# Seven block products for eight in the second feed-forward product of the last chunk

## The chip, the cores and the metric

The kernel runs on one core of a Trainium2 chip. The metric is the device time of one execution in microseconds (us), as the median of several runs. Engines are called as in the profile: PE is the matrix engine (PEld its weight loads), DVE the vector engine, ACT the scalar engine, POOL the GpSimd engine, SP the engine that issues most of the DMAs.

## What is computed

Two layers, each of a sliding attention and a feed-forward product, on 2048 rows of 576 numbers. Both layers use the same weights.

```python
def attention(x, wqkv, wo):          # 32 heads of 18, window of 8 keys, every second row
    q, k, v = split(x @ wqkv)
    logits = q . k[pos - 2 * w] * 18 ** -0.5     # w = 0..7, masked where pos - 2w < 0
    return (softmax(logits) . v) @ wo

def feed_forward(x, w1, w2):         # w1 is 576 x 4608, w2 is 4608 x 576
    return silu(x @ w1) @ w2

for layer in range(2):
    x = x + attention(layernorm(x), wqkv, wo)
    x = x + feed_forward(layernorm(x), w1, w2)
```

## The kernel before

**Stages.** The work is cut into eight chunks, `s` = 0 to 7: four of layer one, four of layer two, each of 512 rows, held as four blocks of 128 rows. `front(s)` makes a chunk's norm, its attention, the projection and a second norm; then comes its feed-forward part. Chunk seven is the last one, and its feed-forward part has no other work beside it. All matmuls take numbers split in two float16 parts, high and low, and add three terms: high by high, high by low, low by high.

**Feed-forward.** Chunks 0 and 1 use plain products (`ffn`). From chunk 2 on `ffn_pairs` takes the 36 tiles of 128 hidden columns as 18 pairs. The first product of a pair is a block product of 2x2 by 2x2 blocks, made with seven block multiplications for eight: `forms` builds seven combinations of the normed rows (split on ACT and DVE, turned by DMA, tiles `xf`, nine of them in the area `xb`), and `prepare` has built seven combinations of w1 per pair, once, kept in device memory (`wfs`) and loaded by `load_wf` into twelve tiles. Each of the products P1 to P7 is seven matmuls of 128x256 (line 1096). Their sums need copies out of the four PSUM banks `zz`: `snap` on ACT (L1100) and `add` on DVE (L1103). SiLU follows on ACT (L1119, L1121, L1123), and then the split of 4x256 hidden numbers into high and low: ACT L1126, DVE L1129.

**The second product** (`second`) runs over groups of three pairs. For each of the four row blocks it adds up 3 pairs x 2 tiles x 3 terms in a PSUM tile `acc`, in two halves of 288 columns (L1151), and DVE adds the sum to x (L861, at the very end L1160). Its weights are tiles of w2, high and low, loaded whole by `load_w2` (L871) into eleven tiles.

**What sets the order.** Each step is handed to `Plan` with an engine, an expected length, what it reads and writes, and a priority; `Plan.order` walks through a model of the engines, lets each free engine take the ready step of lowest priority number, and gives out tile places as they become free. What comes out is a fixed order of instructions on each engine's queue. On the chip an instruction that waits holds all behind it on its queue. Priorities are `s - 1.0` for a chunk's front, `s - 0.5` for feed-forward steps off PE and `s + 0.5` upward for those on PE. So attention and norms of chunk s+1 are worked into the feed-forward part of chunk s.

**Areas.** Tiles of different stages share memory (`area`, `part`, `parts`): a tile can be taken only when no live tile overlaps it. `xa` holds the normed rows for attention, and in the norm before feed-forward also the half `yb` of the combinations; `kvs` holds two tiles of keys and values; `prs` the products of attention; `o` its output or the other half `ya`; `wq` the QKV weights of layer two and two of three tiles `hq`.

Of the kernel before, what the change touches and what calls it, by code (L numbers as in the profile page):

```python
# [264 lines left out]
def sliding_attention_silu_ffn(ctx: ExitStack, tc: tile.TileContext, x, wqkv, wo, w1, w2, out):  # L265
# [10 lines left out]


# [3 lines left out]
    def T(b):  # L281
        return S.tags[b.tag][b.slot]
# [45 lines left out]
    part("yb", XA, 1, [8, KH], F32, turns=False)  # L328
# [15 lines left out]
    parts("yf", [(YH, 0), (YO, 0)], [2, KB], F16)  # L344
# [6 lines left out]
    part("w2", W2A, W2N, [2, D], F16)  # L351
# [64 lines left out]
    dz = accw[:, NP:NP + NP // 2, :].rearrange("p a b -> p (a b)")  # L416
    pace = cp.tile([1, 1], F32, name="pace")
# [57 lines left out]
    highs = []  # L475
    turned = []
# [21 lines left out]
    def layer_norm(xs, prio, into, on_act, on_pe=False, late=[]):  # L498
# [77 lines left out]
    def raw_wq(u):  # L576
# [3 lines left out]
        raw = lambda k: fl(T(rs[k]).bitcast(F32))[:, :QR]  # L580
# [132 lines left out]
    def attention(s, xT, wq, more=None):  # L713
# [4 lines left out]
        for u in range(NU):  # L718
            kv, qt = Buf("kv"), Buf("qt")
            own = [(kv, j) for j in range(NJ)]  # L720
            if wq is None:
# [8 lines left out]
            else:  # L730
                w = wq(u)
                if blk == 0:
# [3 lines left out]
                    op("POOL", 1.86, clear, [], [(kv, "edge")], pr_)  # L736
                else:
# [5 lines left out]
                    op("SP", 0.8, edge, [("eds", lay, par, u)], [(kv, "edge")], pr_, nbytes=20000, lanes=2)  # L743
                for j in range(NJ):
# [31 lines left out]
            keys = own + [(kv, "halo"), (kv, "edge")]  # L776
            lg, pe, mx, sm = Buf("lg"), Buf("pe"), Buf("mx"), Buf("mx")
            for j in range(0, NJ, 2):
# [9 lines left out]
                op("DVE", 2.49, mul, keys + [(qt, j), (qt, j + 1)], [pr], pr_)  # L788
                op("DVE", 2.49, red, [pr], [(lg, j)], pr_)
# [14 lines left out]
            op("DVE", 1.42 if blk == 0 else 0.98, soft_a, [], lgs + [mx], pr_)  # L804
            op("ACT", 0.36, lambda pe=pe, lg=lg: nc.scalar.activation(T(pe), T(lg), AF.Exp, scale=DH ** -0.5),
               lgs, [pe], pr_ - 0.2, table="exp")
            op("DVE", 1.38, soft_b, [], [pe, sm], pr_)
            for j in range(0, NJ, 2):
                pr = Buf("pr")

                for a in range(2):
# [5 lines left out]
                    op("DVE", 1.28, mul, keys + [pe], [(pr, a)], pr_, after=formed[-1:])  # L817
# [6 lines left out]
                op("DVE", 2.55, tree, [], [(pr, 0), (pr, 1), (o, j, u), (o, j + 1, u)], pr_, after=formed[-1:])  # L824
                if s == 0:
                    marks.append(op("POOL", 1.3, lambda j=j, u=u: nc.gpsimd.tensor_copy(
                        pace, T(o)[0:1, j, u * UC:u * UC + 1]), [(o, j, u)], ["pace"], -5))
# [69 lines left out]
    def raw_split(f0, prio):  # L897
# [10 lines left out]
        def rb(f):  # L908
            return fl(T(raws[f][1]).bitcast(F32))
# [428 lines left out]
```

## Time and profile before

| what | value |
|---|---|
| runs | 2142.57 us median of 3 (2138.58 to 2148.47) |
| span of the profiled execution | 2139.6 us; the record has no other time of it |
| POOL, busy in the span | 365.9 us (17%) |
| data moved by DMA | 426.21 MB, mean 199 GB/s |
| matmuls of the second product in chunks 2 to 7 (L1151) | 5184, 669.0 us busy, 286 ns each |
| matmuls of the first product there (L1096) | 5292, 671.2 us busy, 273 ns each |

A matmul's 286 ns is its own length; matmuls follow each other faster than that, since one starts while the one before drains. The time from start to start is read from a stretch of the chain of work with its count of matmuls. In the view of waits, a line names who waited, for whom, the sum in us, how many times, and the longest.

### The profile page before, as it was taken

Reading aid. Unit: us, or ns where it says so; the run is one execution under the profiler, and the core shown is the slowest. Engines: PE = TensorE matmul, PEld = TensorE weight load, DVE = VectorE, ACT = ScalarE, POOL = GpSimd, SP = SyncE. Lnnn points to the kernel's source line nnn. Section 1 sums busy time; section 2 is a strip of 40 time slices with the busy share of each in tenths; the row PEclk is TensorE's granted clock in tenths of the full one; section 3 lists DMA queues with packets and bytes.
Section 4 is the critical chain, followed back from the end, with each engine's and each line's share of the span. In section 5 each row is a group of like instructions: output and inputs, shape, how many; then the busy total and the mean of one; then the engine's idle time right before and its main releaser. Section 6 shows DMA issues by size and latency. Waiting matters only on the chain.

```text
span 2139.6 us, 41351 instructions
## 1 busy us (share of the span) xinstructions
PE 2114.5 (99%) x16233; PEld 1576.2 (74%) x16233; DVE 1640.1 (77%) x2599; ACT 977.0 (46%) x1803; POOL 365.9 (17%) x585
## 2 busy tenths in 40 slices
PE   8999899999999999999999999999999999999999
PEld 5556466656667888877788777887788877888887
DVE  8999999999977997548975599746997569853322
ACT  7555787644254553344424344343443434333332
POOL 2223656234242430001100010000000000000000
PEclk9999999999999999999999999999999999999999
DMA  6576777677799987775748765596565965566551
GB/s 182 154 228 245 250 262 247 197 266 237 197 234 287 325 248 209 175 214 167 211 121 224 201 180 160 138 248 190 157 175 146 250 178 165 162 156 199 152 169 62
DMA packets 334235, 426.21 MB, mean 199 GB/s; under 512 B 145608, under 2 KB 262708, under 8 KB 330072
## 3 DMA queue, kind: packets, MB, share of 16 engines
q1 hardware_dynamic: 293720, 293.19, 49.5%
q0 software_dynamic: 38304, 129.28, 18.8%
q8 instruction: 127, 2.08, 0.4%
q10 hardware_dynamic: 2016, 1.11, 0.2%
q14 instruction: 68, 0.56, 0.1%
HBM read 307.32 MB, written 67.68 MB: 175 GB/s over the span
## 4 chain that ended last, share of the span: by engine, by line
PE 88%; DMA 6%; DVE 3%; issue 1%; ACT 1%; SPq 1%; POOL 0%; ACTq 0%; DVEq 0%; POOLq 0%
PE acc L1151 28%; PE z L1096 13%; PE misc L1096 13%; PE z L1193 9%; PE acc L1212 9%; PE z L682 7%; PE acc L854 5%; PE misc L682 5%; DMA w<-wfs 1%; DMA xb<-yo 1%; DMA h<-in_A_wqkv_dram 1%; DMA w<-in_B_w_dram 1%; DMA w<-w2s 1%; DMA yo<-yh 0%; DMA x<-xd 0%
## 5 line engine op out<-in xcount | busy, mean ns | idle before, releaser
L1151 PE MATMUL acc<-w,h 128*128 128x288 f16 x5184 | 669.0, 286 | 1.6 <-DVE x L861 1.0
L1151 PEld LDWEIGHTS <-h 128*128 128x128 f16 x5184 | 507.2, 98 | 126.8 <-issue 2.2
L1096 PEld LDWEIGHTS <-w 128*128 128x128 f16 x5292 | 517.3, 98 | 72.0 <-DMA w<-wfs 3.7
L1096 PE MATMUL z<-xb,w 128*128 128x256 f16 x2653 | 335.5, 273 | 2.3 <-DMA w<-wfs 1.7
L1096 PE MATMUL misc<-xb,w 128*128 128x256 f16 x2639 | 335.7, 273 | 1.1 <-DVE hs L1103 0.9
L861 DVE SCALAR_TENSOR_TENSOR x<-acc,d,x 128x576 f32<-128x576 f32 x183 | 148.5, 812 | 129.8 <-PE acc L1151 122.2
L1212 PE MATMUL acc<-w,h 128*128 128x288 f16 x1728 | 215.4, 286 | 0.0
L682 PEld LDWEIGHTS <-xa 128*128 128x128 f16 x1344 | 131.0, 98 | 112.9 <-issue 2.1
L1212 PEld LDWEIGHTS <-h 128*128 128x128 f16 x1728 | 168.4, 98 | 44.2
L782 DVE TENSOR_TENSOR prs<-qt,kvs 128x2304 f32<-128x2304 f32 x64 | 163.4, 2552 | 10.3 <-DMA kvs<-kvs 9.4
L815 DVE TENSOR_TENSOR prs<-kvs,pe 128x1152 f32<-128x1152 f32 x128 | 170.8, 1351 | 0.5
L786 DVE TENSOR_REDUCE lg<-prs 128x128 f32<-128x2304 f32 x64 | 163.0, 2547 | 1.0
L822 DVE TENSOR_TENSOR prs<-prs 128x1152 f32<-128x1152 f32 (+1 forms) x128 | 135.1, 1055 | 3.1
L1129 DVE SCALAR_TENSOR_TENSOR h<-wq,sh,h 128x1024 f16<-128x1024 f32 x60 | 76.8, 1280 | 73.3 <-ACT h L1126 73.3
L1193 PE MATMUL z<-xb,w 128*128 128x512 f16 x588 | 129.1, 379 | 3.3 <-ACT w L931 1.6
L682 PE MATMUL z<-wq,xa 128*128 128x432 f16 x658 | 124.4, 346 | 0.0
L854 PE MATMUL acc<-wo,yo 128*128 128x288 f16 x896 | 114.2, 286 | 3.7 <-DMA yo<-yh 2.0
L1100 ACT ACTIVATE wq<-z 128x256 f32<-128x256 f32 x94 | 35.6, 381 | 171.4 <-PE z L1096 171.4
L1193 PEld LDWEIGHTS <-w 128*128 128x128 f16 x588 | 57.3, 98 | 72.0 <-DVE w L933 2.9
L854 PEld LDWEIGHTS <-yo 128*128 128x128 f16 x896 | 87.3, 98 | 27.9 <-DMA yo<-yh 2.8
L763 POOL DMA_DIRECT2D kvs<-kvs x64 | 34.0, 538 | 419.1 <-ACT qt L751 418.9
L682 PE MATMUL misc<-wq,xa 128*128 128x432 f16 x518 | 99.1, 346 | 2.7 <-ACT xa L463 1.3
(229 smaller groups left out, 2578.7 us busy)
## 6 DMA issues: line engine op xcount, KB each, us to landing
w<-wfs SPq DMA_DIRECT2D x756, 160.0 KB, 3.4
w<-w2s SPq DMA_DIRECT2D x252, 288.0 KB, 4.4
wq<-wqs SPq DMA_DIRECT2D x17, 1080.0 KB, 6.2
kvs<-kd POOLq DMA_DIRECT2D x8, 1584.0 KB, 9.2
w<-w1s SPq DMA_DIRECT2D x36, 320.0 KB, 4.3
wfs<-xa POOLq DMA_DIRECT2D x18, 640.0 KB, 4.9
w2s<-w POOLq DMA_DIRECT2D x36, 288.0 KB, 4.1
w1s<-wq POOLq DMA_DIRECT2D x30, 320.0 KB, 4.0
```

Source lines behind the costliest of these rows:

```text
L682: nc.tensor.matmul(T(m)[:, :3 * UC], a, b, start=n == 0, stop=n == len(pl) - 1)
L782: nc.vector.tensor_tensor(T(pr), T(qt)[:, j:j + 2, None, :].to_broadcast([P, 2, W, UC]), win(T(kv), j, 2), op=ALU.mult)
L786: nc.vector.tensor_reduce(T(lg)[:, j:j + 2].rearrange("p a w h -> p (a w h)"), T(pr).rearrange("p a w (h d) -> p (a w h) d", d=DH), axis=A ...
L815: nc.vector.tensor_tensor(T(pr)[:, a].rearrange("p w (h d) -> p w h d", d=DH), v, T(pe)[:, j + a, :, :, None].to_broadcast([P, W, UH, DH]) ...
L822: nc.vector.tensor_tensor(t[:, :, 0:h, :], t[:, :, 0:h, :], t[:, :, h:2 * h, :], op=ALU.add)
L854: nc.tensor.matmul(T(acc)[:, h, 0:288], a, b[:, h * 288:(h + 1) * 288], start=n == 0, stop=n == len(pl) - 1)
L861: nc.vector.scalar_tensor_tensor(t, T(acc)[:, :, 0:288], d, t, op0=ALU.mult, op1=ALU.add)
L1096: nc.tensor.matmul(t, w[:, u, :], v[:, r, :], start=first and m == 0, stop=m == 6, skip_group_check=True)
L1129: op("DVE", 1.2, lambda hq=hq, h=h, sc=sc: nc.vector.scalar_tensor_tensor(T(h)[:, 1].rearrange("p f t -> p (f t)"), T(hq).rearrange("p r t ...
L1151: nc.tensor.matmul(T(acc)[:, h, 0:288], T(hb[t])[:, a, f, j * P:(j + 1) * P], T(wbs[t][f])[:, w, h * 288:(h + 1) * 288], start=t == 0 and ...
L1193: nc.tensor.matmul(T(z), v, u, start=m == 0, stop=m == len(pl) - 1)
L1212: nc.tensor.matmul(T(acc)[:, h, 0:288], T(hb[q])[:, a, j * P:(j + 1) * P], T(wbs[q][0])[:, w, h * 288:(h + 1) * 288], start=q == 0 and m = ...
```

## The change

**The second product of chunk seven** (`S3 = 7`) is made by `ffn_twice` and `seconds`. The hidden numbers of a pair are four blocks: two tiles by two halves of the rows. With the two tiles of w2 in two column halves, they are again 2x2 by 2x2 blocks, and the product takes seven block multiplications for eight. For the left operands POOL makes combinations of the SiLU outputs (L1268: four additions or subtractions of 128x256 per pair), and the split runs over seven rows for four (in two pieces, L1273 on ACT and L1276 on DVE). For the right operands three of seven are the plain halves of w2, and four combinations per pair are made once by `prepare_second`: a load on SP, four subtractions of 128x288 on POOL, one split on ACT and one on DVE, a store on POOL (`wts`). `load_wt` loads each of the seven as a tile of its own, 21 for a group of three pairs, into 24 places in `prs`, `o` and `xa`. In `seconds` each of the seven products runs over the group's three pairs, for two row blocks, in three terms; sums stay in PSUM from one product to the next, with a DVE addition to x (L1316) between.

**Weight forms.** `prepare_second` is called for pairs 0 to 8 behind chunk six's attention and for pairs 9 to 17 behind chunk seven's, with its tiles in `kvs`. The keys and values of chunk seven wait for the store of pair 8 (`hold`).

**Norms.** For chunks four to seven the norm before attention reads its own copy of x, loaded into `prs` once the attention of the chunk before is done, and writes the normed rows in place. The half `yb` of the combinations moves from `xa` to `kvs`, and the second head group of chunks five to seven waits for the norm before it (`free`). The eight x tiles become four double ones.

**Order.** The second product of a chunk's last group gets the priority `pp + SEAM`, that of the next chunk's first products. w2's tiles are kept by column halves. Expected lengths of some steps change.

```diff
+S3 = 7
+LEAD = 0.05
+SEAM = 1.0
...
-    tag("x", 8, [P, D], F32)
+    tag("x", 4, [P, 2, D], F32)
...
-    part("yb", XA, 1, [8, KH], F32, turns=False)
+    part("xp", PR, 1, [NJ, D], F32)
+    parts("yb", [(KV, 0), (KV, KVB)], [8, KH], F32, turns=False)
...
+    parts("h2", [(HA, 0), (HA, FB), (HA, 2 * FB), (W2A, 0), (W2A, FB)], [2, 7, 2 * P], F16)
...
+    parts("q2e", [(WQA, 0), (WQA, 20 * 3 * UC), (W2A, 2 * FB)], [7, 2 * P], F32)
+    parts("wte", [(t, i * WB) for t in (PR, O, XA) for i in range(8)], [2, KH], F16)
+    parts("v2", [(KV, 0), (KV, 10 * WB)], [20 * KH], F16)
...
+            free = formed[-1:] if u == 1 and s > NC else ()
...
+                hold = {S3: [("wts", NP // 2 - 1)], S3 + 1: [("wts", NP - 1)]}.get(s, []) if u < 2 else []
...
-                           [(xT, j)] + [w.keys[5 * h + k] for k in range(a // 3, (b + 2) // 3) for h in range(2)],
-                           [m, (kv, "hold")] if lay else [m], pr_)
+                           [(xT, j)] + hold + [w.keys[5 * h + k] for k in range(a // 3, (b + 2) // 3) for h in range(2)],
+                           [m, (kv, "hold")] if lay else [m], pr_, after=free)
...
+    def prepare_second(q, prio, after):
...
+        op("SP", 0.8, load, ["wsc"], [(b, 0)], prio, nbytes=P * 4 * KH * 4, after=after, lanes=2)
...
+            for r, x, y in ((3, 1, 0), (1, 5, 1), (4, 5, 3), (2, 2, 4)):
+                nc.gpsimd.tensor_tensor(t[:, r], t[:, x], t[:, y], op=ALU.subtract)
+        op("POOL", 3.4, sums, [(b, 0)], [(b, 0)], prio)
+        op("ACT", 1.2, lambda: nc.scalar.activation(split()[:, :, 0, :], rows6()[:, 1:5], AF.Copy, scale=wst[:, q:q + 1]),
+           [(b, 0), "wsc"], [(b, 1)], prio)
+        op("DVE", 1.4, lambda: nc.vector.scalar_tensor_tensor(split()[:, :, 1, :], rows6()[:, 1:5], wst[:, q:q + 1], split()[:, :, 0, :],
+                                                              op0=ALU.mult, op1=ALU.subtract), [(b, 0), (b, 1)], [(b, 1)], prio)
+        op("POOL", 0.57, lambda: nc.gpsimd.dma_start(wts[q], T(b)[:, 12 * KH:]), [(b, 1)], [("wts", q)], prio, nbytes=P * 4 * KH * 4)
...
+    def ffn_twice(s, xf, xs):
...
+                op("ACT", 0.5, lambda hq=hq, d=d: nc.scalar.activation(T(hq)[:, 3], T(hq)[:, 3], AF.Silu, scale=d),
+                   [(hq, 3), "wsc"], [(hq, 3)], pd, table="silu")
+
+                for r, u, v, o in ((4, 6, 3, ALU.add), (5, 4, 0, ALU.subtract), (2, 1, 5, ALU.subtract), (6, 0, 6, ALU.subtract)):
+                    op("POOL", 0.75, lambda hq=hq, r=r, u=u, v=v, o=o: nc.gpsimd.tensor_tensor(T(hq)[:, r], T(hq)[:, u], T(hq)[:, v], op=o),
+                       [(hq, u), (hq, v)], [(hq, r)], pd - 0.01)
+                for r0, r1, sh in ((0, 3, shx), (3, 7, shy)):
...
+    def seconds(s, g, q0, n, hb, xs):
...
+        into = {5: (1, 1), 1: (0, 0), 3: (0, 1), 6: (0, 1), 2: (0, 0), 7: (1, 1), 4: (1, 0)}
+        wb = {(k, t): load_wt(q0 + t, k, s - 0.5, "wt" if s < NL * NC - 1 else "wte") for k in SECOND for t in range(n)}
+        for i, k in enumerate(SECOND):
...
+                                for m, (a, w) in enumerate(((0, 0), (0, 1), (1, 0))):
+                                    nc.tensor.matmul(T(acc)[:, j, 0:KH], T(hb[t])[:, a, row[k], j * P:(j + 1) * P], T(wb[k, t])[:, w, :],
+                                                     start=k in (5, 1, 2) and t == 0 and m == 0, stop=t == n - 1 and m == 2,
+                                                     skip_group_check=True)
...
-                    at = pp + 0.01 * ((g + 1) * n + (j * n + t) // 6) + 0.005
+                    at = (pp + 0.01 * (g + 1) * n if g + 1 < ng else pp + SEAM) + 0.01 * ((j * n + t) // 6) + 0.005
...
-        (ffn if s < S2 else ffn_pairs)(s, XT[s], X[s])
+        (ffn if s < S2 else ffn_pairs if s < S3 else ffn_twice)(s, XT[s], X[s])
...
+        if s in (S3 - 2, S3 - 1):
+            for q in range(*((0, NP // 2), (NP // 2, NP))[s - S3 + 2]):
+                prepare_second(q, s + 0.9, attended[s + 1:s + 2])
```

**How the order moves.** On POOL, between the last key shifts of chunk six (the DMAs from `kvs` to `kvs`) and the first of chunk seven, four output DMAs stand before:

```order
L763 DMA kvs<-kvs 14x864
L1234 DMA out_dram<-x_78 128x576
L1234 DMA out_dram<-x_79 128x576
L1234 DMA out_dram<-x_80 128x576
L1234 DMA out_dram<-x_81 128x576
L763 DMA kvs<-kvs 112x1152
```

After, the nine pairs' subtractions and stores stand there too (the end of them is shown):

```order
L1088 TENSOR_TENSOR kvs<-kvs 128x288 x4
L1094 DMA wts_215<-kvs 128x2304
L1417 DMA out_dram<-x_75 128x576 x2
L1417 DMA out_dram<-x_76 128x576
L1088 TENSOR_TENSOR kvs<-kvs 128x288 x4
L1417 DMA out_dram<-x_76 128x576
L1094 DMA wts_216<-kvs 128x2304
L793 DMA kvs<-kvs 112x1152
```

The store of pair 8 (`wts_216`) has the last output row of chunk five ahead of it on the queue, and chunk seven's shifts behind it.

On ACT, the end of the program before, for the last pair (`wq` holds its hidden numbers, `z` and `misc` are the banks):

```order
L1100 ACTIVATE wq<-misc_103 128x256
L1100 ACTIVATE wq<-z_100 128x256 x2
L1121 ACTIVATE wq<-wq,accw 128x512
L1123 ACTIVATE wq<-wq,accw 128x256
L1119 ACTIVATE wq<-z_100,accw 128x256
L1126 ACTIVATE h<-wq,sh_267 128x1024
```

And after, for the last two pairs (`w_87` is a tile in the area of w2):

```order
L1260 ACTIVATE wq<-z_95,accw 128x256
L1273 ACTIVATE w_87<-wq,shy 128x1024
L1273 ACTIVATE w_87<-wq,shx 128x768
L1241 ACTIVATE w_87<-misc_96 128x256
L1241 ACTIVATE w_87<-z_94 128x256 x2
L1262 ACTIVATE w_87<-w_87,accw 128x2x256
L1264 ACTIVATE w_87<-w_87,accw 128x256
L1260 ACTIVATE w_87<-z_94,accw 128x256
L1273 ACTIVATE h<-w_87,shy 128x1024
L1273 ACTIVATE h<-w_87,shx 128x768
```

The split is two instructions, the larger one first, and both wait for POOL; the snaps of the next pair (L1241) stand behind them.

On SP, where the last chunk begins, the loads of the second product's weights before (`w_93`), among the first product's (`w_70`):

```order
L1071 DMA_TRANSPOSE xb<-yh 128x5x128 x2
L1026 DMA w_70<-wfs_197 128x640
L871 DMA w_93<-w2s_164 128x1152
L871 DMA w_93<-w2s_165 128x1152
L1026 DMA w_70<-wfs_197 128x640
L871 DMA w_93<-w2s_166 128x1152
L1026 DMA w_70<-wfs_198 128x640
```

And after, the first and last rows of a block of 21:

```order
L1066 DMA w_70<-wfs_192 128x640 x3
L1105 DMA prs<-w2s_154 128x576
L1105 DMA prs<-w2s_156 128x576
...
L1105 DMA xa<-wts_209 128x576
L1105 DMA xa<-wts_210 128x576
L1066 DMA w_70<-wfs_193 128x640 x7
```

The loads of the fourth pair (`wfs_193`) stand behind the whole block, where before loads of both kinds took turns.

More of the change, by code (lines that the diff above doesn't have):

```diff
@@ L372, in sliding_attention_silu_ffn @@
     wfs = [tc.dram_tile([P, 7 * KB], F16, name=f"wfs{q}") for q in range(NP)]
+    wts = [tc.dram_tile([P, 4 * 2 * KH], F16, name=f"wts{q}") for q in range(NP)]
     wqs = [tc.dram_tile([P, 30 * UC], F16, name=f"wqs{u}") for u in range(NU)]
@@ L534, in layer_norm @@
                 prio = -19
-            y, yh = Buf("y"), Buf("yh")
+            own = xs[j][0].tag == "xp"
+            y, yh = xs[j] if own else Buf("y"), Buf("yq" if own else "yh")
             def norm(j=j, y=y):
@@ L735, in clear @@
                         nc.gpsimd.memset(T(kv)[0:1, 3:7], 0.0)
-                    op("POOL", 1.86, clear, [], [(kv, "edge")], pr_)
+                    op("POOL", 1.86, clear, hold, [(kv, "edge")], pr_, after=free)
                 else:
@@ L823, in tree @@
                     nc.vector.tensor_tensor(T(o)[:, j:j + 2, u * UC:(u + 1) * UC], t[:, :, 0, :], t[:, :, 1, :], op=ALU.add)
-                op("DVE", 2.55, tree, [], [(pr, 0), (pr, 1), (o, j, u), (o, j + 1, u)], pr_, after=formed[-1:])
+                done = op("DVE", 2.55, tree, [], [(pr, 0), (pr, 1), (o, j, u), (o, j + 1, u)], pd, after=formed[-1:])
                 if s == 0:
@@ L832, in project @@
         pr_ = s - 1.0
+        pd = pr_ if s <= S3 else pr_ - 0.5 + 0.4 + LEAD
         for j in range(NJ):
@@ L845, in project @@
             src = [(o, j, u) for u in range(NU)] + ["so"]
-            op(*(("ACT", 0.7) if s < 2 else ("DVE", 0.45)), hi, src, [(oh, 0)], pr_)
-            op("DVE", 0.86, lo, src + [(oh, 0)], [(oh, 1)], pr_)
-            transposed(oh, lambda oT=oT: T(oT), oT, j, pr_, s < 2)
+            op(*(("ACT", 0.7) if s < 2 else ("DVE", 0.45)), hi, src, [(oh, 0)], pd)
+            op("DVE", 0.86, lo, src + [(oh, 0)], [(oh, 1)], pd)
+            transposed(oh, lambda oT=oT: T(oT), oT, j, pd, s < 2)
             def mm(oT=oT, acc=acc):
@@ L1242, in write_x, with load_x @@
                     op("SP", 0.5, lambda j=j, c0=c0: nc.sync.dma_start(x_rows(out, c, j)[:, c0], T(xs[j])[:, c0]),
-                       [(xs[j], h)], [], pd, nbytes=P * D * 2)
-    def load_x(s, prio, ahead=None):
-        lay, c = divmod(s, NC)
-        xs = [Buf("x") for _ in range(NJ)]
+                       [(*xs[j], h)], [], pd, nbytes=P * D * 2)
+        if s == NL * NC - 1 and S3 < NL * NC:
+            for th, ch in ((0, 1), (0, 0), (1, 1), (1, 0)):
+                for i in range(2):
+                    j, c0 = 2 * th + i, slice(ch * KH, (ch + 1) * KH)
+                    op("SP", 0.38, lambda j=j, c0=c0: nc.sync.dma_start(x_rows(out, c, j)[:, c0], T(xs[j])[:, c0]),
+                       [(*xs[j], ch)], [], pd, nbytes=P * D * 2)
+    def load_x(s, prio, ahead=None, into=None):
+        lay, c = divmod(s, NC)
+        if into is None:
+            halves = [Buf("x") for _ in range(2)]
+            xs = [(halves[j // 2], j % 2) for j in range(NJ)]
+        else:
+            b = Buf(into)
+            xs = [(b, j) for j in range(NJ)]
         for j in range(NJ):
             src = (lambda j=j: x_rows(x, c, j)) if lay == 0 else (lambda j=j: xd[c][j])
-            if ahead:
+            if ahead and lay == 0:
                 op("POOL", 0.54, lambda j=j, src=src: nc.gpsimd.dma_start(T(xs[j]), src()), [], [xs[j]], prio,
@@ L1256, in load_x @@
                 op("SP", 0.41, lambda j=j, src=src: nc.sync.dma_start(T(xs[j]), src()), [("xd", c, j)] if lay else [],
-                   [xs[j]], prio, nbytes=P * D * (4 if s else 5))
+                   [xs[j]], prio, nbytes=P * D * (4 if s else 5), after=ahead or ())
         return xs
```

217 lines of the change are left out of this document (171 added, 46 removed).

## The prediction

> **What bounds the kernel now.** I began with the page's head, to see which engine has no room.
>
> ```profile
> span 2139.6 us, 41351 instructions
> PE 2114.5 (99%) x16233; PEld 1576.2 (74%) x16233; DVE 1640.1 (77%) x2599; ACT 977.0 (46%) x1803; POOL 365.9 (17%) x585
> ```
>
> TensorE is busy in 99% of the span, and nothing else comes near. A busy PE is not yet a PE at its peak, so the next view is that of windows, over the seam between chunks six and seven and over the last chunk.
>
> ```profile
> core 0: us, PE busy (x) PEld busy (x) DVE busy (x) ACT busy (x) POOL busy (x), PEclk, DMA share, GB/s
> 1650.00:1700.00 50.00, 50.00 (x435) 42.34 (x433) 25.54 (x68) 20.63 (x49) 2.22 (x4) 1.00 1.00 268
> 1900.00:1950.00 50.00, 50.00 (x433) 42.00 (x431) 20.21 (x44) 20.48 (x48) 2.22 (x4) 1.00 0.86 223
> 1950.00:2000.00 50.00, 50.00 (x434) 42.27 (x432) 15.78 (x23) 18.25 (x33) 0.00 (x0) 1.00 0.50 153
> 2000.00:2050.00 50.00, 50.00 (x434) 42.22 (x433) 15.72 (x25) 16.78 (x30) 0.00 (x0) 1.00 0.56 167
> ```
>
> PE is full, its granted clock is 1.00, and in the last chunk DVE and ACT are a third busy, POOL idle, the DMA engines half busy. So PE work taken out there is time taken out, as long as the rest keeps up. How much do waits cost? The view of waits, PE alone, from 600 us on:
>
> ```profile
> PE z L1096 <- DMA w<-wfs: 1.7, 2, 1.4
> PE acc L1151 <- DVE x L861: 1.0, 2, 0.8
> PE misc L1096 <- DVE hs L1103: 0.9, 1, 0.9
> PE acc L1151 <- DVE x L1160: 0.6, 1, 0.6
> PE z L1096 <- ACT wq L1100: 0.4, 1, 0.4
> PE misc L1096 <- DMA w<-wfs: 0.2, 1, 0.2
> ```
>
> 4.8 us in all, in six chunks. There is little to win from waits and much to lose by new ones. Last, the end of the chain that ended last:
>
> ```profile
> 2117.05 1.47 PE acc L1151 x12
> 2118.52 0.76 PE z L1096 x7
> 2119.28 14.71 PE acc L1151 x120
> 2134.59 1.64 PE acc L1151 x12
> ```
>
> It gives the price of one matmul of the second product when they follow each other: 14.71 / 120 = 0.1226 us.
>
> **The change part by part.** *Seven block products for eight.* Before, a group of three pairs issues 3 pairs x 2 tiles x 3 terms x 4 row blocks x 2 halves = 144 matmuls of 128x288; after, 7 products x 3 pairs x 2 row blocks x 3 terms = 126 of the same form. Six groups: 864 become 756. 108 x 0.1226 = **-13.2 us**, all of it on the path, since PE is the bound. The first product is as before.
>
> *What the other engines get for it in the last chunk.* Per pair, four additions on POOL (L1268), a split of 7x256 in place of 4x256 numbers, and seven additions to x per group for four.
>
> ```profile
> L1016 DVE SCALAR_TENSOR_TENSOR xa<-wq,accw,xa 128x768 f16<-128x768 f32 x18 | 18.2, 1012 | 0.1
> L1129 DVE SCALAR_TENSOR_TENSOR h<-wq,sh,h 128x1024 f16<-128x1024 f32 x60 | 76.8, 1280 | 73.3 <-ACT h L1126 73.3
> L1197 ACT ACTIVATE h<-hs,sh 128x512 f16<-128x512 f32 x72 | 52.0, 722 | 2.3
> L1126 ACT ACTIVATE h<-wq,sh 128x1024 f16<-128x1024 f32 x60 | 68.9, 1149 | 1.9
> L861 DVE SCALAR_TENSOR_TENSOR x<-acc,d,x 128x576 f32<-128x576 f32 x183 | 148.5, 812 | 129.8 <-PE acc L1151 122.2
> L826 POOL COPY pace<-o x8: 176/1331/2557, 77.1 to 166.7; 1x1 f32<-1x1 f32 x8
> L706 POOL MEMSET hs<- x1: 328/328/328, 1.3 to 1.3; 7x288 f32 x1
> L802 DVE TENSOR_TENSOR pe<-pe,mx 128x256 f32<-128x256 f32 x32 | 13.6, 425 | 1.1
> ```
>
> DVE: 18 x 1.01 for the second split and 18 more additions x 0.81, so 18.2 + 14.6 = 33 us. ACT: 768 numbers lie halfway between 512 and 1024, 0.94 us, x 18 = 17 us. No row shows a POOL addition. From below, a memset of 288 numbers, which reads nothing, takes 0.33. From above, the copy of one number, 0.18 at its shortest, takes up to 2.56 where DVE runs its long two-operand instructions. I take 0.7 for 256 numbers and 0.77 for 288: the memset's work done three times (two reads, a write), nearest to the memset and about twice DVE's 0.425. POOL then has 72 x 0.7 = 50 us. PE needs 49 x 0.109 + 42 x 0.1226 = 10.5 us per pair (0.109 is 0.76 / 7, of the chain's row of seven), 189 us in all. So no engine becomes the bound by its sum.
>
> By its order one can. Along a pair's last steps three POOL additions stand in a row, and a split on ACT and DVE waits for them; behind that split, on the same queue, stand snaps of the next pairs, for which PE waits with a full bank. The copy's spread from 0.18 to 2.56 says that POOL is held while DVE works. The splits keep DVE for 1.28 + 1.01 = 2.3 us of 10.5, so 22% of POOL's additions find it taken, for some 0.6 us: 0.13 each, 0.4 us for three. If a third of that reaches PE: 18 x 0.13 = **+2.4 us**, bounded by 0 and by 18 x 3 x (2.56 - 0.7) = 100. [...]
>
> *The end.*
>
> ```profile
> 2117.55 0.51 ACT L1123 ACTIVATE wq<-wq,accw 128x256 f32<-128x256 f32 x1
> 2119.32 0.47 ACT L1119 ACTIVATE wq<-z,accw 128x256 f32<-128x256 f32 x1 [1.27 <-PE z L1096]
> 2119.83 1.15 ACT L1126 ACTIVATE h<-wq,sh 128x1024 f16<-128x1024 f32 x1
> 2121.01 1.29 DVE L1129 SCALAR_TENSOR_TENSOR h<-wq,sh,h 128x1024 f16<-128x1024 f32 x1 [3.50 <-ACT h L1126]
> 2134.59 1.63 PE L1151 MATMUL acc<-w,h 128*128 128x288 f16 x12 [0.61 <-DVE x L1160]
> ```
>
> Now the last pair's h is whole at 2122.3, and 48 matmuls of the two earlier pairs (5.9 us from 2119.1) cover it. After, on the same clock, three POOL additions run from 2118.1 to 2120.2, ACT's large split to 2121.4, DVE's to 2122.7, the small one to 2123.7. PE has only 24 matmuls to cover it, to 2122.1: a gap of 0.6, six matmuls, a gap of 0.3. The present 0.61 before the last matmuls goes, as each row block has its own bank. Net **+0.4 us**, from -0.1 (POOL at 0.3) to +6.9 (at 2.56).
>
> *Weight forms in chunks six and seven.*
>
> ```profile
> w<-wfs SPq DMA_DIRECT2D x756, 160.0 KB, 3.4
> w<-w2s SPq DMA_DIRECT2D x252, 288.0 KB, 4.4
> wfs<-xa POOLq DMA_DIRECT2D x18, 640.0 KB, 4.9
> ```
>
> Per pair: a load like w2's (4.4), four POOL additions (3.1), 1152 numbers through ACT (1.26) and DVE (1.41, both from the 1024 rows and the slopes above), a store like wfs (4.9): 15 us, two at a time, 68 us for nine pairs. The first nine must be stored before chunk seven's first QKV matmuls. The program's order has 546 first-product and 528 second-product matmuls between chunk six's projection and that place, 546 x 0.109 + 528 x 0.1226 = 124 us. So I count them at nothing; without that cover, PE waits there one for one. The other nine have until group four of the last chunk, over 90 us. Their DVE (13 us) and ACT (11 us) lie in idle time.
>
> *Loads of the last chunk.* 21 tiles of 144 KB per group for six of 288 KB: 3.1 MB for 1.8. Over a group of 31.5 us (3 x 10.5) that is 1.3 MB more, 42 GB/s on 153: some 0.65 of the engines by the window's 0.50. At the seam the first 21 stand on SP as a block ahead of the fourth pair's first-product weights: 3.1 MB at the 268 GB/s of the fullest window is 11.6 us, and those weights land 3.4 later, 15.0. PE has twelve products in hand (12 x 0.76) and 36 second-product matmuls (4.4): 13.5. I take **+0.5 us** (the 1.5 less what SP issues early), from 0 to 6.
>
> *Norms on their own copy, last group after the seam.* Chunks four to seven can start attention sooner, and PE has the old chunk's second product while the new chunk's input is transposed. Cover for the 4.2 us of waits listed above other than the end's; I take **-1.0** (0 to -4.2), as the two DMA waits are not at seams alone. The copy's four loads per chunk pass SP between weights that have slots in hand: nothing.
>
> Sum: -13.2 + 2.4 + 0.4 + 0.5 - 1.0 = -10.9. The profiled execution's span is 2139.6, 1.0 above the fastest run and 3.0 below the median, so it would become 2128.7; on the median of 2142.6 it is **2131.6 us**. 0.5%, about what a measurement of this kernel can tell from no change, is 10.7 us: 2131.9 and 2153.3. The forecast sits on the lower line.
>
> **Rivals.** *All of it, and the seams too* (15%): POOL's additions hide wholly, the end breaks even and 4.2 us of waits go: -13.2 - 4.2 = -17.4, **2125**. For it: from 1663 us on PE now has one wait, the end's.
>
> ```profile
> L1151 PE MATMUL acc<-w,h 128*128 128x288 f16 x1835 | 235.6, 286 | 0.6 <-DVE x L1160 0.6
> L1096 PE MATMUL z<-xb,w 128*128 128x256 f16 x861 | 107.9, 273 | 0.0
> ```
>
> Against: the listed waits are spread over stages that the change only moves.
>
> *Half given back in waits* (24%): QKV of chunk seven waits for the ninth store (its issue on POOL stands behind chunk five's last output row, which waits for PE's own second product), and the block of 21 loads costs its full 6 us rather than 0.5. 2131.6 + 5.5 = **2137**. For it: the DMA engines are at 1.00 and 0.86 in the seam windows already. Against: PE has no wait in either.
>
> *POOL paces the last chunk* (11%): an addition takes the copy's mean of 1.55 rather than 0.7.
>
> ```profile
> L826 POOL COPY pace<-o 1x1 f32<-1x1 f32 x8 | 12.4, 1546 | 64.5 <-DVE o L823 64.5
> ```
>
> Three in a row are 2.6 us later per pair, ACT's split waits, snaps behind it wait, PE with them. Two thirds of 18 x 2.6 reaching PE is 31 us: 2142.6 - 13.2 + 0.4 + 0.5 - 1.0 + 31 = **2160**, slower. It turns slower than before where two thirds of 18 x 3 x (t - 0.7) passes 13.3, at t = 1.07. For it: the copy's row. Against: that copy ran beside DVE instructions of over a microsecond back to back, and DVE is a third busy here.
>
> That the change saves no PE work is no rival: 108 matmuls are counted out of the program.
>
> **How the numbers follow.** The forecast's own case has 50% and reaches from 2127 to 2137; with the line at 2131.9 in its middle, and its cheap side nearer to what the last chunk shows now (one wait), I give 33 of the 50 to faster. With the first rival's 15: faster 0.48. Same: the other 17 and the second rival's 24, 0.41. Slower: 0.11. The range takes in the first and second rival, some drift of the median (its three runs span 10 us) and the seam's 6 us on top of the POOL term: 2122 to 2146, leaving the POOL rival out.
>
> **What would show it.** Right: 756 matmuls at the new second product's line, back to back at 0.12; PE waits in the last chunk under 4 us; POOL's additions at 0.6 to 0.9; a gap of about a microsecond after the last first product. Wrong: PE waits on ACT's snaps or on h in every pair (POOL's rival), one long wait at chunk seven's first QKV or at the fourth pair's weights (the second), or a PE time that fell by 13 with a span that did not.

## The result and the profile after

The changed kernel takes 2155.7 us (median of seven runs, 2148.1 to 2161.3) beside 2141.2 for the kernel before, measured with it. The ratio is 1.0063, with a 95% interval from 1.0046 to 1.0080: slower by 13.5 us, where 10.9 less was forecast. The profiled execution has a span of 2151.0 us, 11.4 more than before; it is one of the faster executions, with a mean granted clock of 0.997 where most of the others show 0.994 or 0.995. Its head:

```profile
span 2151.0 us, 41793 instructions
PE 2106.6 (98%) x16125; PEld 1567.9 (73%) x16125; DVE 1709.5 (79%) x2657; ACT 1010.5 (47%) x1839; POOL 493.4 (23%) x747
```

The instruction count shows the change at work: 16233 - 16125 = 108 matmuls fewer, POOL from 585 to 747 instructions. PE is still the bound, but its share fell from 99 to 98%, so it now waits. For whom, the view of waits says, PE alone from 600 us on:

```profile
PE misc L1176 <- ACT wq L1180: 4.3, 2, 3.4
PE z L1176 <- DMA xb<-yo: 4.0, 1, 4.0
PE z L1176 <- DMA xb<-yh: 3.7, 1, 3.7
PE misc L1176 <- DMA xb<-yh: 2.0, 1, 2.0
PE z L1376 <- ACT h L1378: 1.9, 1, 1.9
PE z L1237 <- DMA w<-wfs: 1.8, 1, 1.8
PE z L1237 <- ACT w L1241: 1.5, 2, 1.0
PE misc L1176 <- DVE wq L1183: 1.2, 1, 1.2
PE acc L1334 <- DVE x L894: 1.2, 1, 1.2
PE acc L1307 <- DVE x L1316: 0.9, 1, 0.9
PE acc L887 <- DVE x L894: 0.5, 1, 0.5
PE misc L1176 <- DVE h L1183: 0.5, 1, 0.5
PE z L1176 <- DMA w<-wfs: 0.4, 1, 0.4
```

(Line numbers have moved: first product 1096 to 1176, and 1237 in the last chunk; second product 1151 to 1334, and 1307 in the last chunk; snap 1100 to 1180 and 1241; addition to x 861 to 894.) With two more rows of 0.2 us in the last chunk (one on `xb`, one on the snap L1241) the sum is 24.3 us, where it was 4.8. The windows show what these waits bring with them: two around the seams before chunks four and five, one where the weight forms begin, one in the last chunk.

```profile
core 0: us, PE busy (x) PEld busy (x) DVE busy (x) ACT busy (x) POOL busy (x), PEclk, DMA share, GB/s
1150.00:1170.00 20.00, 16.05 (x118) 11.85 (x116) 5.19 (x10) 6.46 (x15) 3.70 (x7) 0.91 0.96 245
1410.00:1430.00 20.00, 16.33 (x112) 11.42 (x110) 5.24 (x13) 7.60 (x19) 2.12 (x4) 0.91 0.98 246
1590.00:1610.00 20.00, 15.44 (x120) 12.39 (x118) 18.55 (x40) 6.94 (x13) 6.31 (x9) 0.91 0.75 225
1950.00:2000.00 50.00, 47.02 (x405) 39.28 (x403) 24.20 (x32) 23.60 (x38) 26.04 (x32) 1.00 0.95 290
```

A granted clock of 0.91 over 20 us is 1.8 us of work lost. That gives the account of the span: -13.2 for the matmuls, 24.3 - 4.8 = +19.5 for waits, 3 x 1.8 = +5.4 for the clock behind three of them, in sum +11.7; the span shows +11.4. (The first 600 us, left out of it, have 15.9 us of PE waits, where they had 16.6.) So nothing speaks against the saving being there in full. What came on top is waits, most of them in three places.

**The seams.** PE's own timeline at the seam before chunk four, in the changed kernel:

```profile
1156.78 0.93 PE L1176 MATMUL z<-xb,w 128*128 128x256 f16 x7
1157.55 1.63 PE L1334 MATMUL acc<-w,h 128*128 128x288 f16 x12
1163.13 1.65 PE L1176 MATMUL z<-xb,w 128*128 128x256 f16 x7 [3.95 <-DMA xb<-yo]
1164.58 8.21 PE L1334 MATMUL acc<-w,h 128*128 128x288 f16 x60
```

A first product of the new chunk waits 3.95 us for its turned input, and behind it on the queue stand 60 matmuls of the old chunk's last group, none of which waits when its turn comes. The product itself then takes 1.65 us instead of 0.93, at half clock (granted 0.50 from 1163 to 1166 us, 1.00 from 1166 on).

**Where the weight forms begin.** The same view in the changed kernel, DVE's rows, then POOL's, then ACT's:

```profile
1595.83 0.16 DVE L517 TENSOR_TENSOR nt<-nt 128x4 f32<-128x4 f32 x1
1596.02 0.65 DVE L518 TENSOR_TENSOR nt<-nt 128x4 f32<-128x4 f32 x1
1596.71 0.17 DVE L519 TENSOR_SCALAR nt<-nt 128x4 f32<-128x4 f32 x1
1596.91 0.80 DVE L520 TENSOR_TENSOR nt<-nt 128x4 f32<-128x4 f32 x1
1597.74 0.72 DVE L521 SCALAR_TENSOR_TENSOR nt<-nt 128x4 f32<-128x4 f32 x1
...
1595.83 0.82 POOL L1088 TENSOR_TENSOR kvs<-kvs 128x288 f32<-128x288 f32 x1 [3.71 <-DMA kvs<-in_B_w_dram]
1596.90 2.41 POOL L1088 TENSOR_TENSOR kvs<-kvs 128x288 f32<-128x288 f32 x3 [0.25 <-DMA kvs<-in_B_w_dram]
...
1592.16 1.25 ACT L1090 ACTIVATE kvs<-kvs,accw 128x1152 f16<-128x1152 f32 x1 [3.96 <-POOL kvs L1088]
1600.69 0.44 ACT L1141 ACTIVATE yo<-o 128x288 f16<-128x288 f32 x1 [7.28 <-DVE o L1132]
```

DVE works through steps of the norm on four numbers, 0.16 us each. From 1596.02 on, beside POOL's additions, three of them take 0.65 to 0.80, up to the length of one such addition (0.82); L519 runs in POOL's pause between two additions (1596.65 to 1596.90) and takes its 0.17. The norm's rows come late, ACT's queue stands 7.28 us for them (L1141), and the snap that PE waits for stands behind that: the list's 3.4 us on L1180. These three steps make up 1.7 us of it (2.17 for 0.48); the rest is work that DVE has back to back. Earlier ACT stood 3.96 us for POOL itself.

It happens to other DVE steps too, here 15 us earlier:

```profile
1579.19 0.70 DVE L512 TENSOR_SCALAR nt<-mv 128x4 f32<-128x4 f32 x1
1579.93 0.71 DVE L513 TENSOR_SCALAR nt<-nt 128x4 int32<-128x4 int32 x1
1578.18 3.33 POOL L1088 TENSOR_TENSOR kvs<-kvs 128x288 f32<-128x288 f32 x4 [1.81 <-DMA kvs<-in_B_w_dram]
```

Both have a median of 0.17 over their seven executions. An estimate of all of it: each DVE instruction after 1000 us that overlaps one of these additions (L1088), against the median of its line and form without one, gives 13.7 us of longer DVE time in all.

**The last chunk.** The block of loads (1.8 us on `wfs`) and the late snaps (L1241, 1.5 + 0.2). POOL's and ACT's groups in the changed kernel:

```profile
L1088 POOL TENSOR_TENSOR kvs<-kvs 128x288 f32<-128x288 f32 x72 | 67.0, 941 | 180.5 <-DMA kvs<-in_B_w_dram 124.3 <-DVE yh L874 53.8
L1268 POOL TENSOR_TENSOR wq<-wq 128x256 f32<-128x256 f32 x48 | 35.1, 744 | 68.7 <-ACT wq L1264 64.6 <-ACT wq L1260 3.1
L1090 ACT ACTIVATE kvs<-kvs,accw 128x1152 f16<-128x1152 f32 x18 | 22.5, 1251 | 29.4 <-POOL kvs L1088 28.2 <-DMA prs<-wts 0.8 <-DVE nt L517 0.3
```

The additions of the last chunk take 0.74 us (the other 24, on tiles in w2's area, 0.73), as estimated (0.7). Those of the weight forms take 0.94 in the mean instead of 0.77, and ACT stood 28.2 us for them.

### The profile page after: what moved, and what is told of

It reads as the page before. It is cut to its first block, busy times and chain, and to the rows that moved or that the text cites. A ratio compares the mean times of both kernels' runs of the same rounds, so it can differ in the third digit from the quotient of the medians.

```text
span 2151.0 us, 41793 instructions
## 1 busy us (share of the span) xinstructions
PE 2106.6 (98%) x16125; PEld 1567.9 (73%) x16125; DVE 1709.5 (79%) x2657; ACT 1010.5 (47%) x1839; POOL 493.4 (23%) x747
## 4 chain that ended last, share of the span: by engine, by line
PE 81%; DMA 8%; DVE 6%; issue 2%; ACT 1%; POOL 1%; SPq 0%; ACTq 0%; DVEq 0%; POOLq 0%
PE acc L1334 22%; PE z L1176 11%; PE misc L1176 10%; PE z L710 8%; PE z L1376 6%; PE acc L1395 6%; PE misc L710 5%; PE acc L887 4%; PE acc L1307 4%; PE z L1237 2%; PE misc L1237 2%; DMA xb<-yh 2%; DMA w<-w2s 1%; DMA w<-wfs 1%; DMA wq<-in_B_w_dram 1%
## 5 line engine op out<-in xcount | busy, mean ns | idle before, releaser
L1334 PE MATMUL acc<-w,h 128*128 128x288 f16 x4320 | 558.0, 287 | 1.2 <-DVE x L894 1.2
L1334 PEld LDWEIGHTS <-h 128*128 128x128 f16 x4320 | 423.6, 98 | 105.3 <-issue 1.4
L1176 PEld LDWEIGHTS <-w 128*128 128x128 f16 x4410 | 432.4, 98 | 76.7 <-issue 15.9
L1176 PE MATMUL z<-xb,w 128*128 128x256 f16 x2261 | 289.2, 274 | 8.2 <-DMA xb<-yo 4.0
L1176 PE MATMUL misc<-xb,w 128*128 128x256 f16 x2149 | 275.2, 273 | 8.1 <-ACT wq L1180 4.3
L1395 PE MATMUL acc<-w,h 128*128 128x288 f16 x1728 | 215.6, 286 | 2.1 <-DMA w<-w2s 2.1
L710 PEld LDWEIGHTS <-xa 128*128 128x128 f16 x1344 | 131.0, 98 | 112.7 <-issue 2.1
L1395 PEld LDWEIGHTS <-h 128*128 128x128 f16 x1728 | 168.4, 98 | 46.5 <-issue 2.5
L894 DVE SCALAR_TENSOR_TENSOR x<-acc,d,x 128x576 f32<-128x576 f32 x160 | 129.4, 811 | 83.2 <-PE acc L1334 77.4
L813 DVE TENSOR_TENSOR prs<-qts,kvs 128x2304 f32<-128x2304 f32 x64 | 163.3, 2552 | 5.3 <-ACT qts L781 4.1
L710 PE MATMUL z<-wq,xa 128*128 128x432 f16 x602 | 114.7, 346 | 0.0
L710 PE MATMUL misc<-wq,xa 128*128 128x432 f16 x574 | 110.3, 346 | 2.7 <-ACT xa L489 1.3
L1088 POOL TENSOR_TENSOR kvs<-kvs 128x288 f32<-128x288 f32 x72 | 67.0, 941 | 180.5 <-DMA kvs<-in_B_w_dram 124.3
```

Of the source, the lines that this page charges most:

```text
L710: nc.tensor.matmul(T(m)[:, :3 * UC], a, b, start=n == 0, stop=n == len(pl) - 1)
L813: nc.vector.tensor_tensor(T(pr), T(qt)[:, j:j + 2, None, :].to_broadcast([P, 2, W, UC]), win(T(kv), j, 2), op=ALU.mult)
L894: nc.vector.scalar_tensor_tensor(t, T(acc)[:, :, 0:288], d, t, op0=ALU.mult, op1=ALU.add)
L1176: nc.tensor.matmul(t, w[:, u, :], v[:, r, :], start=first and m == 0, stop=m == 6, skip_group_check=True)
L1334: nc.tensor.matmul(T(acc)[:, h, 0:288], T(hb[t])[:, a, f, j * P:(j + 1) * P], T(wbs[t][f])[:, h, w, :], start=t == 0 and f == 0 and m == 0 ...
L1395: nc.tensor.matmul(T(acc)[:, h, 0:288], T(hb[q])[:, a, j * P:(j + 1) * P], T(wbs[q][0])[:, h, w, :], start=q == 0 and m == 0, stop=q == n ...
```

## The experiments

Each ratio is to runs of the kernel before, measured beside it; differences in us are the ratio's, worked out on 2142.6. The first theories were A (the order at the seams) and B (the own copy moves attention's first steps to the seam).

**Each part undone.** The new place of the last group, the norms' own copy, or the seven products:

```diff
# e1, e3: place undone
-at = (pp + 0.01 * (g + 1) * n if g + 1 < ng else pp + SEAM) + 0.01 * ((j * n + t) // 6) + 0.005
+at = pp + 0.01 * ((g + 1) * n + (j * n + t) // 6) + 0.005
# e2, e3: copy undone
-layer_norm(load_x(s, s - 1.0, attended[-1:], into="xp"), s - 1.0, "xa", False, ...)
+layer_norm(X[s], s - 1.0, "xa", False, ...)
# e4: eight products, no weight forms
-S3 = 7
+S3 = 8
```

> The changed kernel with one edit taken back: the second product of a chunk's last group gets its old priority, so on PE it stands ahead of the next chunk's products again. Theory A, the order at the seams: in the changed kernel's profile PE waits 4.1 and 3.8 us at the seams before chunks four and five for turned inputs, and each wait is followed by 3.4 us at half clock (1.7 us lost): 11.4 us, of which the kernel before has 1.8. These go: about 10 us less than the changed kernel, some 2146 us. Theory B, the norms' own copy moved QKV and the key shifts to the seam, and the turning DMAs are late for that: the waits stay, at other instructions, and the time within 3 us of the changed kernel's 2155.7.

> The changed kernel with the norm before attention reading x itself again, not its own copy. Theory B: QKV and key shifts leave the seams, the waits there go, about 10 us less than the changed kernel, 2146 us. Theory A: the seams keep their waits, as the order there is the same, 2153 to 2157 us.

> Both edits taken back: old priority at the seams and no own copy, so the seven products and their weight forms are what is left. Both theories: seam waits as in the kernel before. What then remains is 13.2 us of PE work saved, against waits beside the weight forms (about 9 us in the changed profile from 1570 to 1752) and in the last chunk (about 5): 2141, no change against before. If the weight forms' waits came from the other two edits (theory C denied), 2132.

> The changed kernel with eight products in the last chunk and no weight forms: own copy and new order at the seams are what is left. Theories A and B: the two seams still cost about 10 us, 2151 us. If the weight forms were the whole loss: 2139 to 2142, as before.

Measured: e1 1.0091 (1.0072 to 1.0110), e2 1.0133 (1.0115 to 1.0151), e3 1.0166 (1.0149 to 1.0182), e4 1.0066 (1.0049 to 1.0083). No forecast of the first three held: taking away a part that should cost made things worse. For e4 10 us over the kernel before were forecast and 14 came. The waits of PE in the last chunk of e1, its longest row:

```profile
PE misc L1237 <- DMA w<-wfs: 8.8, 1, 8.8
```

and of e3:

```profile
PE misc L1237 <- DMA xb<-yo: 19.8, 3, 16.8
PE misc L1237 <- DMA w<-wfs: 6.6, 1, 6.6
```

With the old place and without the copy the last chunk's input forms come 17 us late, since chunk seven's attention stands behind the weight forms: its QKV products (L710) begin within 3 us of the landing of the ninth store, at 1764 us in e3 and 1718 in the changed kernel, and end at 1853 and 1806. With the copy (e1), the new place (e2) or both that store lands at 1735, 1754 and 1718 us, with neither at 1761. At the seams of 1150 to 1500 us theory A's mechanism did hold: e1 has no wait for `xb` there. And e4, which saves nothing and makes no weight forms, has such waits before chunks four, five and six (from 1100 us on):

```profile
PE z L1176 <- DMA xb<-yo: 4.9, 1, 4.9
PE misc L1176 <- DMA xb<-yo: 4.3, 1, 4.3
PE z L1176 <- DMA xb<-yh: 4.3, 2, 3.2
```

**One part at a time, without seven products.** The same edits, all with `S3 = 8`; and the changed kernel with the weight forms free:

```diff
# f4_forms_free, load_wt
-src = wts[q][:, i * n:(i + 1) * n]
+src, key = w2s[2 * q + (i > 1)][:, n:2 * n] if i < 3 else w2s[2 * q][:, 0:n], ("w2s", 2 * q + 1)
# and at the call of prepare_second
-if s in (S3 - 2, S3 - 1):
+if False:
```

> The changed kernel with all three parts undone: eight block products in the last chunk, no weight forms, the old place of the last group, the norms on x itself. What stays of the change is the layout (x in halves, shared areas, new durations in the planner's table). Theory C (the new place of the last group makes first products wait at the seams): 2143 us, like before. Theory D (the own copy makes the seams late): 2143 us as well. Rival E (the layout and the planner's new table alone reshuffle the order and cost what the other runs showed): 2155 us or more.

> Only the own copy is left of the change (eight products, no weight forms, old place of the last group). Theory C: 2143 us, and PE waits at the seams before chunks four to seven of under 1.5 us each. Theory D: 2155 us, with waits of 3 to 5 us at those seams. Rival E: like the run with nothing left, whatever that shows.

> Only the new place of the last group is left of the change (eight products, no weight forms, norms on x itself). Theory C: 2155 us, with PE waits of 3 to 5 us in first products at the seams before chunks four to seven. Theory D: 2143 us. Rival E: like the run with nothing left.

> The changed kernel without the making of the weight forms: the last chunk's weight loads read as many bytes of the stored second-product weights in their place (the last chunk's second product takes other weights; its work is the same). If the forms cost the 10 us of waits and half clock that the changed kernel shows from 1550 to 1800 us: 2146 us, and under 1 us of waits there. If those waits are the seams' lateness, which would show elsewhere: 2155 us as before, with waits at the seam before chunk six or seven in their place.

Measured: f1 1.0009 (1.0000 to 1.0019), f2 1.0051 (1.0030 to 1.0072), f3 1.0051 (1.0036 to 1.0066), f4 1.0012 (1.0001 to 1.0023). So the layout costs nothing that can be told, and rival E is out. Theory C's time came for the new place (f3, +11 us), though not with waits of 3 to 5 us: f3's waits on `xb` sum to 6.6 us from 600 us on, none over 2.0. But the copy alone costs as much (f2, whose runs spread from 2141 to 2165). In its profile that is not theory D's late seam but another wait, 4.7 us on `wfs` at 1457 us, with 3.4 us of clock behind it. So C and D are each half right. Us over the kernel before, by ratio:

| | neither | new place | own copy | both |
|---|---|---|---|---|
| eight products | +2 (f1) | +11 (f3) | +11 (f2) | +14 (e4) |
| seven products | +36 (e3) | +28 (e2) | +20 (e1) | +14 (the change) |

In the upper row place and copy cost 12 us together; in the lower they save 22. And f4 gives the price of making the weight forms: 1.0063 against 1.0012, 11 us. The waits of PE from 1555 to 1800 us, in the changed kernel the first, eighth, ninth, eleventh and thirteenth row of the list above (7.6 us), are in f4 one:

```profile
PE misc L1176 <- DMA xb<-yo: 3.5, 1, 3.5
```

It is the seam's kind again, now before chunk six. f4's order is another one, so the 11 us are not all in this stretch: its profile has 9.1 us less of waits than the changed kernel's, 4.1 of them here.

**Other places for the work.** g1 starts the weight forms only when the next chunk's input forms are done; g2 keeps the new place to the last two seams; g3 is both; g4 is g3 with the block of loads spread.

```diff
# g1, g3, g4
-prepare_second(q, s + 0.9, attended[s + 1:s + 2])
+prepare_second(q, s + 0.9, formed[-1:])
# g2, g3, g4: the old priority unless
+... if g + 1 < ng or s < S3 - 2 else pp + SEAM + 0.01 * ((j * n + t) // 6) + 0.005
# g4 (and h1, below)
-load_wt(q0 + t, k, s - 0.5, ...)
+load_wt(q0 + t, k, s - 0.45, ...)
```

> The changed kernel, all of the work in it; only the weight forms start later, once the next chunk's input forms are made (DVE is 46 of 50 us busy at the old place, about half of it behind). Theory F (the forms cost 10 us because their DVE and ACT steps stand among attention and input forms in a stretch in which DVE is full): 2146 us, and PE waits from 1560 to 1800 us of under 2 us in all where the changed kernel has about 9. Rival G (POOL's additions stretch DVE's instructions and hold ACT wherever they stand): 2155 us, the waits moved to the new place.

> The changed kernel; only the new place of the last group is kept to the last two seams (before chunks six and seven), the others have the old one. Theory C (the new place costs 8 us at the seams before chunks four and five, and the last seam needs it): 2148 us, no PE wait over 1.5 us from 1150 to 1500 us, and the last seam as in the changed kernel (under 1 us of waits from 1900 to 1960). Rival H (any other order only moves the waits on): 2155 us or more.

> Both of these together. If both theories hold and the two add: 2155.7 - 10 - 8 = 2138 us, 4 us under the kernel before. If only one of them holds: 2146 to 2148. If neither: 2155.

> Both together, and the second product's weight loads of the last chunk stand behind the first product's in priority, so that the block of 21 loads is spread. If the 2 us wait for the fourth pair's weights in the changed kernel is the block's: 2 us under the run with both alone, about 2136, and no PE wait for a wfs load after 1960 us. Rival: the loads only land later for the second product, which then waits: the same as the run with both, or more.

Measured: g1 1.0241 (1.0227 to 1.0255), g2 1.0125 (1.0104 to 1.0145), g3 1.0273 (1.0249 to 1.0298), g4 1.0197 (1.0180 to 1.0214). In g1 the waits from 1555 to 1800 us fell to 1.3, as theory F had it, but chunk seven's QKV stands behind the ninth store (landed at 1799 us, QKV from 1801), its attention starts late, and the last seam pays (PE's waits of g1 from 1900 us, the three longest):

```profile
PE z L1237 <- DMA xb<-yh: 15.6, 2, 14.6
PE acc L887 <- DMA yo<-yh: 9.7, 1, 9.7
PE z L1237 <- DMA w<-wfs: 4.4, 1, 4.4
```

So neither of the two places is free: early the forms stand in DVE's full stretch, late they hold the last chunk back. In g2 the early waits for `xb` went and others came (`wfs` 4.1 at 944 us, 4.7 at 1207, 7.4 in the last chunk): rival H. g3 was the slowest of all. g4 against g3 shows the block: g3 has 5.3 us on `wfs` from 1900 us on, g4 none. Its profiled span is 7.4 us shorter, 5.3 of it that wait, with a mean granted clock of 0.990 for 0.987; by ratio it is 16 us, which that wait does not explain.

**What in the weight forms costs.** All engines keep the changed kernel's order in h2 and h3; only lengths differ. h4 is the changed kernel with the copy in chunks six and seven only, the new place at the last seam only, and h1's spread.

```diff
# h2_one_sum (the loads put the rows at 1 to 4)
-for r, x, y in ((3, 1, 0), (1, 5, 1), (4, 5, 3), (2, 2, 4)):
+for r, x, y in ((0, 1, 2),):
# h3_short_split, on ACT and in the same way on DVE
-nc.scalar.activation(split()[:, :, 0, :], rows6()[:, 1:5], ...)
+nc.scalar.activation(split()[:, 0:1, 0, :], rows6()[:, 1:2], ...)
# h4_late_only
+load_x(..., into="xp") if s >= S3 - 1 else X[s]
+... if g + 1 < ng or s < S3 - 1 else pp + SEAM
```

> The changed kernel; only the second product's weight loads of the last chunk stand behind the first product's in priority, so that the block of 21 is spread. If the block is the 2 us wait for weights at 1968 us: 2153.5 us and no PE wait on a wfs load after 1960 us. Rival (DMA engines are simply full there): the wait stays or moves to the second product, 2155.7.

> The changed kernel with one of the four POOL additions per pair left in the making of the weight forms (the loaded rows stand where the sums would; planner's numbers, so every engine's order, unchanged). Theory P (POOL's additions stretch DVE's instructions and hold ACT's split): 2146 us, waits from 1560 to 1800 us under 2 us. Rival Q (the time of ACT's and DVE's splits in a stretch in which DVE is full): 2154 us.

> The changed kernel with ACT's and DVE's splits of the weight forms on 288 of their 1152 numbers (the store sends the first row four times; order unchanged). Theory P: 2154 us. Rival Q: 2146 us, waits from 1560 to 1800 us under 2 us. If either alone is enough to take the lateness away, both runs show 2146 to 2149.

> All work of the changed kernel; the own copy only in chunks six and seven, the new place of the last group only at the last seam, and the spread of the first kernel of this call. If own copy and new place cost where they aren't needed and help where the last chunk's forms come late: 2155.7 - 8 (seams) - 2 (block) = 2146 us. Rival (every order moves the waits on, the making of forms delays chunk seven's attention): 2155 us or more, with waits before the last chunk's first products.

Measured: h1 1.0039 (1.0024 to 1.0055), h2 1.0009 (0.9997 to 1.0022), h3 1.0035 (1.0014 to 1.0056), h4 1.0051 (1.0030 to 1.0071). h2, which leaves out three of four additions, gives back 11.6 us, as much as f4: 54 additions of about a microsecond on an engine that is idle for three quarters of the span. (By the profiled spans it is 6.9 us.) Its two longest waits from 1555 to 1800 us:

```profile
PE misc L1176 <- ACT wq L1180: 2.0, 2, 1.3
PE misc L1176 <- DVE wq L1183: 1.1, 1, 1.1
```

The waits of the stretch fall to 3.6 us in all (theory P had under 2), and the half clock is gone (1.00 from 1590 to 1610). In h3 4.7 us of them stay (its longest row):

```profile
PE misc L1176 <- ACT wq L1180: 3.6, 2, 3.0
```

That is theory P: the estimate of DVE's longer time falls from 13.7 us to 3.3 in h2 and stays at 14.0 in h3. The splits may not be free either: h3 came out halfway, 6 us faster than the change by ratio, but its runs go from 2141 to 2167 and the two intervals overlap. h1's interval overlaps the change's, and 1.4 us on `wfs` stays at another product: whether the spread helps there is open. h4 is as slow as its rival had it, 2155.8, by waits in other places.

**A version of it.** The additions on DVE (1.9 us per pair in the planner's table); i2 has h4's edits too.

```diff
-nc.gpsimd.tensor_tensor(t[:, r], t[:, x], t[:, y], op=ALU.subtract)
+nc.vector.tensor_tensor(t[:, r], t[:, x], t[:, y], op=ALU.subtract)
```

> The changed kernel, all work done; only the additions of the weight forms run on DVE in place of POOL, with 1.9 us per pair in the planner's table. Theory P' (POOL as their place costs: 3.2 us and more per pair against under 2 on DVE, DVE and POOL holding each other): 2147 us, waits from 1560 to 1800 us of under 3 us. Rival Q' (DVE is full in that stretch, any work added there comes out at PE): 2155 us or more, with waits on DVE's or ACT's steps from 1560 to 1800 us of 9 us or more.

> The additions on DVE, and with them the own copy only in chunks six and seven, the new place of the last group only at the last seam, and the weight loads spread. If the parts add: 2155.8 - 9 = 2147 us against the run without the additions moved, and about 2142, level with the kernel before, if the small waits for loads also go; the full saving would be 2130. Rival: 2155 us, the waits again in other places.

Measured: i1 1.0047 (1.0030 to 1.0065), i2 1.0069 (1.0050 to 1.0089). In i1, all work done, the waits of 1555 to 1800 us are

```profile
PE acc L887 <- DMA yo<-yh: 0.9, 1, 0.9
PE z L1176 <- DMA xb<-yh: 0.8, 1, 0.8
PE misc L1176 <- ACT wq L1180: 0.6, 1, 0.6
```

2.3 us for 7.6: with all work done, the stretch loses its waits once the additions leave POOL. ACT's standing for the additions does not make these waits by itself: it stands 28.4 us for them in i1, now for DVE, and 28.2 in the changed kernel. But the last chunk now waits 3.0 on `wfs` and 2.6 on ACT and DVE, so the time is 2151 where theory P' had 2147: 3.4 us less than the changed kernel by ratio, with intervals that overlap. i2 came out as its rival had it, 2157.9. No version with seven products beat the kernel before.

## Why the prediction was wrong

**Seven products, -13.2: right.** With it, the waits and the clock behind them the span closes to within half a microsecond.

**POOL and ACT in the last chunk, +2.4: right in size.** Additions at 0.73 to 0.74 (0.7 was taken), late snaps 1.5 + 0.2 us. The longest of them is the described kind: at 1998 us ACT's split stands 2.37 us for L1268, and PE 0.99 for the snap behind it. But it comes in three places and not in every pair. POOL does not pace the last chunk; the rival that ended slower named the wrong place.

**The end, +0.4: right in size, by luck.** The wait of 0.6 on L1160 was to go and two gaps for the last pair's h were to come. Neither happened: PE never waits for h there, and a wait of the old kind, for an addition to x (L1316), is 0.9.

**Weight forms: the step that failed first.** "So I count them at nothing" rested on 124 us of cover ahead of chunk seven's QKV, and "Their DVE (13 us) and ACT (11 us) lie in idle time". PE indeed never waits at QKV (L710) in the list. But the nine pairs did not take 68 us: from the first load at 1555 us to the landing of the ninth store at 1718 it is 163, and QKV begins right behind it. Nor was the idle time there. The stretch in which the first pairs are made, in the kernel before:

```profile
1555.00:1605.00 50.00, 50.00 (x432) 42.03 (x431) 48.10 (x56) 21.63 (x35) 0.00 (x0) 1.00 0.58 169
```

DVE is 48.10 of 50 us busy. The prediction had read 1650 to 1700, where it is 25.54, and its DVE and ACT sums left POOL's effect on them out. Measured: 11 us (f4), all of it gone by ratio without three of four POOL additions (h2). DVE's load alone is not the cause: i1 puts the additions on DVE as well, and the waits of this stretch fall from 7.6 us to 2.3.

**Seams, own copy, last group, -1.0: failed, with the wrong sign.** "PE has the old chunk's second product while the new chunk's input is transposed" would be so if a free engine chose on the chip. But the order is fixed by a model: where the model has the transposes done in time, the first product is put ahead of the second product's matmuls, and where the chip's are late, these stand behind a waiting instruction (60 of them behind the 3.95 us at 1163 us). That is read from the order and the waits, not from the model's own times. Over the kernel before, the new place alone costs 11 us (f3), the copy 11 (f2), both 14 (e4), 2 of them the layout's (f1); in the changed kernel's profile it is 4.0 + 3.7 + 2.0 of waits (before chunks four, five and three) and 3.6 of clock. That they cover the late last chunk (22 us, lower row of the table) had not been seen at all.

**Loads, +0.5: mis-sized.** 1.8 us on the weights behind the block, inside the bounds of 0 to 6; up to 8.8 where the seam's order differs (e1).

Not settled: what makes each single order come out with waits at one seam and not at another. Every edit of a priority moved some.

## What to carry to other kernels

In a kernel whose matrix engine is full and whose queues are ordered ahead by a model, price an added step by the stretch it lands in, engine by engine, and not by the engines' shares of the span; and look at what it holds up on other engines and on its queue. A filler helps only if it stands ahead of the instruction that may wait: here 60 matmuls stood behind a wait of 3.95 us. Before trusting a saving of half a per cent, undo the parts one by one in both directions: here two parts that cost 12 us without the third save 22 with it.

## What the runs showed of the hardware

In the changed kernel waits of 3.4 to 4.0 us on PE were each followed by a stretch at half clock (0.91 over 20 us; taken finer, 0.50 for 3.4 us), so that a wait of 4 costs nearly 6 here; the waits of 2.0 at 899 us and of 1.8 at 1969 us were not (1.00 from 900 to 960 and from 1950 to 2000). Other runs do not divide so. In f3 a stretch with a single wait, of 2.0 us, shows the lower clock, as its waits

```profile
PE misc L1176 <- DMA xb<-yh: 2.0, 1, 2.0
```

and its windows show:

```profile
1150.00:1170.00 20.00, 18.04 (x142) 14.57 (x140) 5.76 (x13) 7.20 (x15) 2.95 (x4) 0.91 0.98 257
```

In f4 a wait of 3.4 us, from 1421 us on, was not followed by such a stretch:

```profile
1420.00:1440.00 20.00, 16.64 (x123) 11.83 (x122) 12.91 (x8) 4.34 (x9) 1.14 (x2) 1.00 0.76 226
```

Between the two, length alone does not tell in these runs which wait brings the half clock.

POOL's additions held up the smallest DVE instructions most for their length: beside them, four numbers took 0.65 to 0.80 us for 0.16 (L518, L520 and L521, which read two operands), and L512 and L513, which read one, were held as long (0.70 and 0.71 for 0.17). The longest L1209, with 1024 numbers, took 1.75 for 1.28. h2 shows what the additions are worth here: 11.6 us by ratio for three of four.
